# Attention scores turned onto key partitions, the maximum by way of TensorE, the quotient taken after the values

## The chip, the cores and the metric

One core of one Trainium2 chip runs the whole program. The metric is the device time of a launch in microseconds (us); the kernel before has a median of 992.38 us over 3 runs (990.18 to 994.85).

## The reference

Attention with the queries averaged in pairs, then a gated MLP on the tokens. There are 4 batches of 8 heads, 1152 keys and 576 averaged queries each, a head dimension of 64; the MLP goes from 512 to 2048 and back. All data is float32.

```python
q_pool = q.reshape(B, H, S // 2, 2, D).mean(axis=3)
scores = (1.0 / np.sqrt(D)) * np.matmul(q_pool, k.transpose(0, 1, 3, 2))
scores = scores - np.max(scores, axis=-1, keepdims=True)
attn = np.exp(scores)
attn = attn / (np.sum(attn, axis=-1, keepdims=True) + 1e-09)
x = np.matmul(attn, v)                      # then heads side by side: 2304 tokens x 512
h = x @ w_in                                # 2304 x 2048
g = h * np.clip(h + 3.0, 0.0, 6.0) / 6.0
return (g @ w_out).astype(np.float32)
```

The keys and queries are scaled by about 7.9 before, so the scores spread widely and the maximum matters.

## The kernel before, in words

**Precision.** A matmul on plain float32 is recorded as two matmul instructions. Where that is avoided, an operand is split into a rounded high part and a low part of type float32r (`upper_k`/`lower_k`, `take_q`, `split_x`, `convert`, `upper`/`lower`), and two or three products of rounded parts are added in PSUM.

**Attention.** The work goes by 16 pairs of heads (`g`). Keys and queries of a pair are loaded, pooled or split, turned by TensorE (`turn_k`, `turn_q`) and copied out of PSUM. A tile of scores has 128 queries on the partitions and 1152 keys along the row: nine tiles a pair, one of which (`None`) holds 64 queries of either head, its other half filled with zeros. `scores` makes a tile in three chunks of 384 keys. `least` (L392) moves a chunk out of PSUM, scaled by minus the scale, and carries the running minimum along the row; `expo` (L401) takes the exponential with that minimum as a bias and sums the row on the way; `recip` and `normal` (L407 to L412) divide the row by its sum on GpSimd. `turn` (L423) turns the result, 128 x 128 at a time, because the value product needs keys on partitions, and `take` (L306, L308) copies it into `pt`. `values` (L448) multiplies `pt` by the values, both heads side by side in one PSUM bank, for 320 or 256 queries at a time. `split_x` and `spill` write the two parts of x to DRAM.

**MLP.** Tokens go in chunks of 256 while attention runs: `layer` (L172, 12 matmuls of 256 columns), a gate on ScalarE and VectorE (L177, L181, L185, L190), and `project` (L205, 6 matmuls of 512 columns), for 16 blocks of 128 hidden features a chunk. One block of one chunk is one step `m`; there are 96. The last 768 tokens follow behind attention (L707 to the end). Before that, each block of weights is loaded raw, split into rounded parts by seven instructions (`convert`, L484 to L514, half of a block at a time) and written back to DRAM.

**Order.** The order of all instructions before L707 is written by the class `Order`: each step has a place (a priority), an estimated cost on its engine, the steps that it needs, and the buffers that it takes and frees. A list is worked through as if these estimates were times, and the order that comes out is held on every engine by dependencies. So each engine has one fixed queue. The constants at the top set the places: a pair lies 27 places after the one before it, block `f` of the weights at place 6 + 12.5 f, the MLP steps begin at place 112 and follow at 6.4 and later 3.15 places. SP issues all DMAs in its own place of that order.

**Buffers.** Up to the tile `WIDE` the scores have two double banks of PSUM (tag `v`), after it two single ones; the transposes have two banks, value products and weight splitting share one (tag `av`). `pt0` and `pt1` are single, score rows `s` have five buffers.

Of the kernel before, what the change touches and what calls it, by code (L numbers as in the profile page):

```python
# [113 lines left out]
def pooled_attention_then_gated_mlp(ctx, tc, q, k, v, w_in, w_out, out):  # L114
# [3 lines left out]
    P = 128  # L118
# [12 lines left out]
    REST = SQ % P  # L131
    QW = 2 * REST + SQ - REST
# [55 lines left out]
    def lower(pool, r6, gh, n):  # L188
        gl = pool.tile([P, n], F32R, tag="gl", name="gl")
        nc.vector.tensor_tensor(out=gl, in0=r6, in1=gh.bitcast(F32), op=ALU.subtract)  # L190
        return gl
# [46 lines left out]
    def second_part(early):  # L238
        front.close()
        ps_m["s"] = early.enter_context(tc.tile_pool(name="ps_s", bufs=2, space=PSUM))  # L240
# [4 lines left out]
    with ExitStack() as a:  # L245
        ld = a.enter_context(tc.tile_pool(name="ld", bufs=2))
        kq = a.enter_context(tc.tile_pool(name="kq", bufs=4 * KT // KC))
        sp = a.enter_context(tc.tile_pool(name="sp", bufs=5))
        sm = a.enter_context(tc.tile_pool(name="sm", bufs=6))
        tp = a.enter_context(tc.tile_pool(name="tp", bufs=1))  # L250
        vp = a.enter_context(tc.tile_pool(name="vp", bufs=2))
        xo = a.enter_context(tc.tile_pool(name="xo", bufs=2))
        ps_tr = a.enter_context(tc.tile_pool(name="ps_tr", bufs=2, space=PSUM))
        ps_av = a.enter_context(tc.tile_pool(name="ps_av", bufs=1, space=PSUM))

        q_t = []
        for n in range(2):
            both = []  # L260
            for nm in ("qh", "ql"):
                t = const.tile([P, 2, QW], F32R, name=f"{nm}{n}")
                for j in range(2):
                    z = slice(REST * (1 - j), REST * (2 - j))
                    nc.vector.tensor_copy(out=t[:, j, z], in_=zero.to_broadcast([P, REST]))
                both.append(t)
            q_t.append(both)

        TILES = [(None, 0)] + [(j, n) for n in range(SQ // P) for j in range(2)]
        EARLY = [(0, 0), (0, 1), (None, 0), (1, 0), (1, 1)] + TILES[5:]
        NTI = len(TILES)
        GROUPS = ((0, REST + 2 * P), (REST + 2 * P, SQ - REST - 2 * P))

        def tiles(g):
            return TILES if g else EARLY
# [3 lines left out]
        ps_t, s_t, cm_t, den_t, pt_t, av_t, xo_t = {}, {}, {}, {}, {}, {}, {}  # L281
# [44 lines left out]
        def near(g):  # L326
            return (ps_w, "tx") if g < NEAR else (ps_tr, "tr")

# [36 lines left out]
        def bank(i):  # L365
            return "v" if i < WIDE else "s"

# [395 lines left out]
```

## Time and profile before

| | |
|---|---|
| median of the runs | 992.38 us |
| span of the profiled execution, first to last instruction | 988.8 us |
| what a run's median has beyond that span | 3.6 us |
| PE (TensorE matmuls) busy | 942.5 us, 95%, 6288 instructions |
| DVE (VectorE) busy | 590.6 us, 60% |
| ACT (ScalarE) busy | 532.6 us, 54% |
| POOL (GpSimd) busy | 362.2 us, 37% |
| read from and written to DRAM | 171.97 and 30.93 MB |

Busy times are unions of instruction times. Matmuls overlap in the pipeline and their ends are modelled, so a PE that is shown busy is not one at its best pace; the distance from one matmul to the next is the better measure. The profile counts each plain float32 matmul of the value product as two records. For the profiled execution no time of its own is listed beside the span, so the median stands for it.

### The profile page before, as it was taken

What the parts mean: (1) busy time and instruction counts of PE and PEld (TensorE: products, weight loads), DVE (VectorE), ACT (ScalarE), POOL (GpSimd) and SP (SyncE); (2) the same over time, 40 slices, a digit from 0 to 9 for tenths busy, and PEclk for the clock granted to TensorE, in tenths of its full rate; (3) what the DMA queues carried; (4) which work ended last, traced back from release to release, by engine and by line L of the source; (5) the groups of instructions that cost most, each with busy time, mean ns of one, the idle gap of its engine ahead of it and who ended that gap; (6) DMA issues with size and microseconds to landing.
All of it is one profiled execution on the core that took longest, in us unless ns stands there. A gap on an engine that the chain in (4) does not pass through costs nothing.

```text
span 988.8 us, 17816 instructions
## 1 busy us (share of the span) xinstructions
PE 942.5 (95%) x6288; PEld 783.6 (79%) x6288; DVE 590.6 (60%) x1752; ACT 532.6 (54%) x1098; POOL 362.2 (37%) x338
## 2 busy tenths in 40 slices
PE   5898997999999999999999999999999999999997
PEld 4676676677678888888888878888898887788886
DVE  5787788678687766566575756566565552222222
ACT  4786786666565656455564555455564542222222
POOL 3876867545565434333251423323121110000000
PEclk9999997999999999999999999999999999999999
DMA  5875565788777476568475766557565668633332
GB/s 174 274 231 192 178 202 174 227 288 287 265 252 240 153 224 199 183 207 285 159 252 163 235 223 217 200 176 276 185 226 168 223 229 283 219 127 126 127 124 85
DMA packets 80888, 204.06 MB, mean 206 GB/s; under 512 B 7840, under 2 KB 31392, under 8 KB 80800
## 3 DMA queue, kind: packets, MB, share of 16 engines
q1 hardware_dynamic: 80800, 202.93, 62.6%
q8 instruction: 50, 0.82, 0.3%
q14 instruction: 38, 0.31, 0.1%
HBM read 171.97 MB, written 30.93 MB: 205 GB/s over the span
## 4 chain that ended last, share of the span: by engine, by line
PE 80%; DVE 9%; DMA 5%; ACT 3%; issue 2%; POOL 1%; SPq 0%; ACTq 0%; DVEq 0%; POOLq 0%
PE ph L172 18%; PE po L205 15%; PE pav L448 14%; PE pqk L384 13%; PE ptp L423 11%; PE pt L205 4%; DVE s L392 3%; DMA w<-w_d 3%; PE ptk L333 2%; PE ptq L346 1%; DVE gl L190 1%; DMA raw<-in_moe_w_in_dram 1%; DMA raw<-in_moe_w_out_dram 1%; ACT s L401 1%; DVE pcv L503 1%
## 5 line engine op out<-in xcount | busy, mean ns | idle before, releaser
L412 POOL TENSOR_SCALAR s<-s,den 128x1152 f32<-128x1152 f32 x144 | 177.8, 1235 | 340.1 <-DVE den L408 204.9
L423 PE MATMUL ptp<-ident,s 128*128 128x128 f32 x1296 | 209.1, 277 | 8.3 <-ACT pt L306 4.8
L401 ACT ACTIVATE s<-s,cm 128x1152 f32<-128x1152 f32 x144 | 181.7, 1262 | 40.7 <-DVE s L392 39.6
L384 PE MATMUL pqk<-kT,qh 128*128 128x384 f32 x480 | 184.9, 402 | 6.3 <-DVE s L392 5.2
L172 PE MATMUL ph<-mxmxh,w 128*128 128x256 f32 x896 | 184.3, 289 | 6.0 <-DMA w<-w_d 4.9
L423 PEld LDWEIGHTS ptp<-ident,s 128*128 128x128 f32 x1296 | 156.6, 142 | 39.2 <-issue 9.6
L306 ACT COPY pt<-ptp 128x384 f32<-128x384 f32 x296 | 138.7, 481 | 77.3 <-PE ptp L423 75.0
L392 DVE TENSOR_SCALAR_CACHE_REDUCE s<-pqk,cm 128x384 f32<-128x384 f32 x248 | 151.0, 609 | 32.0 <-PE pqk L384 27.7
L384 PE MATMUL pqk<-kT,ql 128*128 128x384 f32 x480 | 156.8, 343 | 0.0
L172 PEld LDWEIGHTS ph<-mxmxh,w 128*128 128x128 f32 x896 | 147.1, 191 | 11.5 <-DMA w<-w_d 4.5
L448 PE MATMUL pav<-pt,vr 128*64 128x256 f32 (+1 forms) x1152 | 149.2, 410 | 0.1
L205 PE MATMUL po<-w,gh 128*128 128x512 f32 x448 | 140.6, 395 | 0.0
L177 ACT ACTIVATE r<-ph,three 128x256 f32<-128x256 f32 (+1 forms) x128 | 63.8, 499 | 142.2 <-PE ph L172 141.9
L172 PE MATMUL ph<-mxmxl,w 128*128 128x256 f32 x448 | 126.7, 283 | 0.0
L448 PEld LDWEIGHTS pav<-pt,vr 128*64 128x64 f32 x1152 | 78.9, 137 | 56.7 <-issue 6.2
L181 DVE SCALAR_TENSOR_TENSOR r<-r,ph 128x256 f32<-128x256 f32 (+1 forms) x128 | 57.6, 450 | 97.8 <-ACT r L177 97.2
L308 DVE COPY pt<-ptp 128x384 f32<-128x384 f32 x136 | 74.9, 553 | 56.3 <-PE ptp L423 55.8
L392 DVE TENSOR_SCALAR_CACHE_REDUCE s<-pqk 128x384 f32<-128x384 f32 (+1 forms) x144 | 95.4, 662 | 16.6 <-PE pqk L384 15.0
L384 PEld LDWEIGHTS pqk<-kT,qh 128*128 128x128 f32 x480 | 89.1, 193 | 16.1 <-DVE s L392 11.4
L205 PE MATMUL po<-w,gl 128*128 128x512 f32 x224 | 93.5, 417 | 6.8 <-DVE gl L190 3.5
L205 PEld LDWEIGHTS po<-w,gh 128*128 128x128 f32 x448 | 84.8, 189 | 14.8
L190 DVE TENSOR_TENSOR gl<-r,gh 128x256 fp32r<-128x256 f32 (+1 forms) x128 | 79.1, 618 | 28.7 <-ACT gh L185 28.2
(55 smaller groups left out, 1132.8 us busy)
## 6 DMA issues: line engine op xcount, KB each, us to landing
w<-w_d SPq DMA_DIRECT2D x224, 512.0 KB, 4.6
w_d<-scratch SPq DMA_DIRECT2D x32, 512.0 KB, 3.7
kr<-in_k_dram SPq DMA_DIRECT2D x32, 288.0 KB, 4.6
qr<-in_q_dram SPq DMA_DIRECT2D x32, 288.0 KB, 4.8
vr<-in_v_dram SPq DMA_DIRECT2D x16, 576.0 KB, 5.3
raw<-in_moe_w_in_dram SPq DMA_DIRECT2D x16, 512.0 KB, 4.3
raw<-in_moe_w_out_dram SPq DMA_DIRECT2D x16, 512.0 KB, 4.3
mxmxh<-xh_d SPq DMA_DIRECT2D x7, 512.0 KB, 6.1
```

The source lines that it names most:

```text
L172: nc.tensor.matmul(ps, w[:, wi, cs], x[:, c, :], start=(m == 0), stop=(m == 3 * NCC - 1))
L177: nc.scalar.activation(out=r6, in_=ps, func=AF.Relu, bias=three)
L190: nc.vector.tensor_tensor(out=gl, in0=r6, in1=gh.bitcast(F32), op=ALU.subtract)
L205: nc.tensor.matmul(o, g[:, ts], w[:, wi, :], start=(f == 0 and n == 0), stop=(f == NFC - 1 and n == 2))
L306: nc.scalar.copy(out=out, in_=in_)
L308: by[eng].tensor_copy(out=out, in_=in_)
L384: nc.tensor.matmul(ps, x, kk.rearrange("p t k -> p (t k)"), start=(m == 0), stop=(m == len(ops) - 1))
L392: nc.vector.tensor_scalar(out=s[:, c * NK:end * NK].rearrange("p (c k) -> p c k", k=NK), in0=ps_t.pop((i, c))[0][:, 0:end - c, 0:NK], scal ...
L401: nc.scalar.activation(out=s, in_=s, func=AF.Exp, bias=cm_t.pop(i)[:, KC - 1:], scale=-1.0, accum_out=den_t[i])
L412: nc.gpsimd.tensor_scalar(out=s, in0=s, scalar1=den_t.pop(i), scalar2=1.0, op0=ALU.mult, op1=ALU.mult)
L423: nc.tensor.transpose(ps[:, x, :], s_t[i][:, o:o + P], ident)
L448: nc.tensor.matmul(av[j * D:(j + 1) * D, :], vr_t[g][:, j, t, :], pt_t[g, gr][:, t, j, :], start=(t == 0), stop=(t == KT - 1),)
```

## The change

Scores are made with keys on the partitions, so that what leaves the exponential is already what the value product needs, and `turn` and `take` go. A pair is cut into three thirds (`h`) of 192 queries, both heads side by side: one tile of scores has 128 keys by 2 x 192 queries, nine tiles a third, four matmuls of 192 columns each.

- `keep` (ACT) copies each tile out of PSUM; `most` (DVE) keeps a running maximum over the nine tiles, element by element.
- `fold`, `best`, `spread`: the maximum is turned by TensorE so that queries lie on partitions, reduced over the 128 that remain (DVE), and turned back from a broadcast operand, so that every partition holds the maximum of each query.
- `lessen` (DVE) subtracts it in place from three tiles at a time, `expo` (ACT) takes the exponential with the scale, without a bias and without a sum.
- `total` (POOL) adds up exponentials over tiles: two additions of 1152 columns that leave three tiles for the first six pairs, two more of 384 columns that leave one tile for the later ten. `denominators` sums over partitions with a matrix of ones, and so leaves the sum on every output row.
- `values` is as before, on 192 queries. `guard`, `recip`, `divide` take the quotient on its result; the low part of x is made by POOL and not by DVE.

The order has new steps and costs; a pair lies 26.9 places after the one before it, weight block `f` at place 13 + 9.3 f, MLP steps from place 99.5 in steps of 6.95 and 3.07, a projection 3.5 places behind its layer and not 1. POOL may take the gate's low half instead of DVE at a handicap of 12 places. PSUM has three banks for scores, one for the maximum, one for value products, three for turning keys and queries in the first four pairs and then the MLP's three.

```diff
-REC, NRM, TRN = 4, 4.5, 7
-AVL = 2
-FIRST, STEPS, LAG = 112, (6.4, 3.15), 1
-CONV, CSTEP = 6, 12.5
-NEAR = 5
-WIDE = 40
+SBUFS = 4
+FIRST, STEPS, LAG = 99.5, (6.95, 3.07), 3.5
+CONV, CSTEP = 13, 9.3
+NEAR = 4
+ADDS = (2, 4, 6)
+CUT = 2
+PER, AT, NGL = 26.9, (5.4, -6.8, 2.4, 14.5, -50, 27, 15.4), 12
...
+def adds(g, h):
+    return ADDS[0] if g < ADDS[2] else ADDS[1]
...
+        def scores(eng, g, h, t):
+            ps = ps_t[g, h, t] = ps_s.tile([P, 2, HQ], F32, tag="s", name="pqk")
+            for j in range(2):
+                for m, w in enumerate(q_t[g, h]):
+                    nc.tensor.matmul(ps[:, j, :], kT[g, j][:, t, :], w[:, j, :], start=(m == 0), stop=(m == 1))
+        def keep(eng, g, h, t):
+            if t == 0:
+                s_t[g, h] = sp.tile([P, KT, 2, HQ], F32, tag="s", name="s")
+            copy(eng, s_t[g, h][:, t], ps_t[g, h, t])
+        def most(eng, g, h, t):
+            if t == 1:
+                m_t[g, h] = sm.tile([P, 2, HQ], F32, tag="m", name="m")
+            m = m_t[g, h]
+            nc.vector.tensor_tensor(out=m, in0=ps_t[g, h, t], in1=s_t[g, h][:, 0] if t == 1 else m, op=ALU.max)
+        def fold(eng, g, h):
+            st = st_t[g, h] = ps_st.tile([P, 2 * TQ, P], F32, tag="m", name="pst")
+            m = m_t.pop((g, h)).rearrange("p j (t q) -> p (j t) q", q=QP)
+            for x in range(2 * TQ):
+                nc.tensor.transpose(st[:QP, x, :], m[:, x, :], ident)
+        def best(eng, g, h):
+            m_t["q", g, h] = sm.tile([QP, 2 * TQ], F32, tag="mq", name="mq")
+            nc.vector.tensor_reduce(out=m_t["q", g, h], in_=st_t[g, h][:QP], axis=AX.X, op=ALU.max)
+        def spread(eng, g, h):
+            mq = m_t.pop(("q", g, h))
+            st = st_t[g, h] = st_t[g, h].rearrange("p x k -> p (x k)")[:, 0:2 * HQ]
+            for x in range(2 * TQ):
+                nc.tensor.transpose(st[:, x * QP:(x + 1) * QP], mq[:, x:x + 1].to_broadcast([QP, P]), ident[:QP, :QP])
+        def third(g, h, c):
+            return s_t[g, h][:, KC * c:KC * (c + 1)].rearrange("p t j q -> p t (j q)")
+        def lessen(eng, g, h, c):
+            s = third(g, h, c)
+            nc.vector.tensor_tensor(out=s, in0=s, in1=st_t[g, h].unsqueeze(1).to_broadcast([P, KC, 2 * HQ]), op=ALU.subtract)
+        def expo(eng, g, h, c):
+            s = third(g, h, c)
+            nc.scalar.activation(out=s, in_=s, func=AF.Exp, scale=SCALE)
+        def total(eng, g, h, n):
+            if n == 0:
+                d_t[g, h] = dp.tile([P, KC, 2 * HQ], F32, tag="d", name="d")
+            d = d_t[g, h]
+            if n < 2:
+                out, x, y = d, third(g, h, 0) if n == 0 else d, third(g, h, n + 1)
+            else:
+                out, x, y = d[:, 0], d[:, 0], d[:, n - 1]
+            by[eng].tensor_tensor(out=out, in0=x, in1=y, op=ALU.add)
+        def denominators(eng, g, h, t0, t1):
             if t0 == 0:
+                pv = ps_av.tile([P, 512], F32, tag="av", name="pav")
+                av_t[g, h] = pv[:, HQ:2 * HQ], pv[:, 0:HQ]
+            den = av_t[g, h][0]
+            n = adds(g, h)
+            d = d_t.pop((g, h)).rearrange("p t (j q) -> p t j q", j=2) if n else s_t[g, h]
+            last = {0: KT, 2: KC, 4: 1}[n]
+            for t in range(t0, t1):
+                for j in range(2):
+                    nc.tensor.matmul(den[j * D:(j + 1) * D, :], ones, d[:, t, j, :], start=(t == 0), stop=(t == last - 1))
+        def values(eng, g, h, t0, t1):
+            av = av_t[g, h][1]
             for t in range(t0, t1):
                 for j in range(2):
                     nc.tensor.matmul(
+                        av[j * D:(j + 1) * D, :], vr_t[g][:, j, t, :], s_t[g, h][:, t, j, :],
                         start=(t == 0), stop=(t == KT - 1),
                     )
+        def guard(eng, g, h):
+            x_t[g, h] = xo.tile([P, HQ], F32, tag="x", name="x")
+            nc.scalar.activation(out=x_t[g, h], in_=av_t[g, h][0], func=AF.Copy, bias=EPS)
+        def recip(eng, g, h):
+            nc.vector.reciprocal(out=x_t[g, h], in_=x_t[g, h])
+        def divide(eng, g, h):
+            x = x_t[g, h]
+            nc.vector.tensor_tensor(out=x, in0=av_t.pop((g, h))[1], in1=x, op=ALU.mult)
+
...
+        def split_x(eng, g, h):
...
+                by[eng].tensor_tensor(out=xl, in0=x_t.pop((g, h)), in1=xh.bitcast(F32), op=ALU.subtract)
...
+                    add(("mm", g, h, t), z + t * step, {"PE": (376, 590)}, partial(scores, g=g, h=h, t=t),
+                        ([("mm", g, h, t - 1)] if t else [("mm", g, h - 1, KT - 1)] if h else [("mm", g - 1, NH - 1, KT - 1)] if g else [])
+                        + ([("el", g, h)] if not t else [])
+                        + [("ek", g, j, t // KC) for j in range(2)],
+                        ("sa", "sb"), (("q",) + (("kT", "kT") if h == NH - 1 else ())) if t == KT - 1 else ())
+                    add(("cp", g, h, t), z + t * step, {"ACT": (360, 440)}, partial(keep, g=g, h=h, t=t),
+                        [("mm", g, h, t)] + ([("cp", g, h, t - 1)] if t else []), () if t else ("S",), ("sa",) if t else ("sa", "sb"))
+                    if t:
+                        add(("mx", g, h, t), z + t * step + .1, {"DVE": (480, 560)}, partial(most, g=g, h=h, t=t),
+                            [("mm", g, h, t), ("mx", g, h, t - 1) if t > 1 else ("cp", g, h, 0)], ("m",) if t == 1 else (), ("sb",))
+                z += THIRD
+                add(("s1", g, h), z + AT[2], {"PE": (440, 660)}, partial(fold, g=g, h=h), [("mx", g, h, KT - 1)], ("st",), ("m",))
+                add(("s2", g, h), z + AT[2], {"DVE": (610, 690)}, partial(best, g=g, h=h), [("s1", g, h)])
+                add(("s3", g, h), z + AT[2], {"PE": (330, 550)}, partial(spread, g=g, h=h), [("s2", g, h)])
                 for c in C3:
+                    add(("su", g, h, c), z + AT[3] + 2 * c, {"DVE": (1280, 1360)}, partial(lessen, g=g, h=h, c=c),
+                        [("s3", g, h), ("cp", g, h, KT - 1)] + ([("su", g, h, c - 1)] if c else []), (), ("st",) if c == 2 else ())
+                    add(("ex", g, h, c), z + AT[3] + 1 + 2 * c, {"ACT": (1160, 1260)}, partial(expo, g=g, h=h, c=c), [("su", g, h, c)])
+                na = adds(g, h)
+                for n in range(na):
+                    cost = 2890 if n < 2 else 1040
+                    add(("ad", g, h, n), z + AT[4] + 2 * n, {"POOL": (cost, cost + 20)}, partial(total, g=g, h=h, n=n),
+                        [("ex", g, h, c) for c in (range(2) if n == 0 else (2,) if n == 1 else ())] + ([("ad", g, h, n - 1)] if n else []),
+                        () if n else ("d",))
+                z += AT[6] if na else AT[5]
+                parts = {0: KT, 2: KC, 4: 1}[na]
+                cuts = (0, 3, 6, KT) if g < CUT else (0, KT)
+                jobs = [(denominators, x, min(x + 3, parts)) for x in range(0, parts, 3)]
+                jobs += [(values, x, y) for x, y in zip(cuts, cuts[1:])]
+                for n, (fn, t0, t1) in enumerate(jobs):
+                    cost = 320 * (t1 - t0) + (190 if g < CUT or n == 0 else 0)
+                    add(("av", g, h, n), z + n, {"PE": (cost, cost + 220)}, partial(fn, g=g, h=h, t0=t0, t1=t1),
+                        [("av", g, h, n - 1)] if n else [("ad", g, h, na - 1) if na else ("ex", g, h, 2), ("lv", g)],
+                        () if n else ("av",), (("S",) + (("d",) if na else ()) + (("vr",) if h == NH - 1 else ()))
+                        if n == len(jobs) - 1 else ())
                 z += n
+                add(("gu", g, h), z + 1, {"ACT": (270, 350)}, partial(guard, g=g, h=h), [("av", g, h, len(jobs) - 1)], ("x",))
+                add(("rc", g, h), z + 1, {"DVE": (270, 340)}, partial(recip, g=g, h=h), [("gu", g, h)])
+                add(("dv", g, h), z + 1, {"DVE": (280, 360)}, partial(divide, g=g, h=h), [("rc", g, h)], (), ("av",))
+                add(("xh", g, h), z + 2, {"ACT": (260, 340)}, partial(split_x, g=g, h=h), [("dv", g, h)], ("xo",))
+                add(("xl", g, h), z + 2, {"POOL": (580, 600)}, partial(split_x, g=g, h=h), [("xh", g, h)], (), ("x",))
...
-            add(("gl", m), z, {"DVE": (400, 490)}, partial(do_lower, m=m), [("gh", m)], (), ("r6",))
+            add(("gl", m), z, {"DVE": (400, 490), "POOL": (740, 760, NGL)}, partial(do_lower, m=m), [("gh", m)], (), ("r6",))
```

## Rows read from the trace of the kernel before

**Rows 1.** Chain of waits cut to two stretches, 50 to 188 and 344 to 826 us, by line.
```profile
by line: PE pav L448 23.6%; PE ptp L423 15.7%; DVE s L392 13.7%; PE pqk L384 13.4%; DVE pcv L503 4.9%; issue 4.9%; DMA raw<-in_moe_w_out_dram 4.0%; DVE scratch L507 3.5%; DVE pcv L498 2.5%; DVE pt L308 2.5%; PE ptk L333 2.2%; DVE ql L357 1.
...
by line: PE po L205 22.1%; PE ph L172 19.2%; PE pqk L384 17.4%; PE pav L448 16.9%; PE ptp L423 15.3%; DVE gl L190 2.2%; PE ptk L333 1.8%; PE ptq L346 1.5%; DVE s L392 1.0%; issue 0.7%; ACT pt L306 0.4%; ACT s L401 0.4%; ACT gh L185 0.3%; DV
```

**Rows 2.** Windows by stage: length; PE, PEld, DVE, ACT, POOL busy; clock, DMA share, GB/s.
```profile
50.00:188.00 138.00, 125.97 (x868) 95.08 (x864) 104.32 (x297) 102.42 (x210) 99.72 (x98) 0.96 0.60 194
...
344.00:826.00 482.00, 477.68 (x3381) 407.86 (x3379) 290.56 (x922) 260.68 (x544) 149.68 (x129) 1.00 0.65 213
826.00:988.80 162.80, 153.95 (x797) 131.47 (x795) 44.23 (x82) 43.56 (x82) 0.00 (x0) 0.98 0.46 150
```

**Rows 3.** Windows by stage, line 384 alone: length, PE and PEld busy (instructions).
```profile
50.00:188.00 138.00, 59.40 (x222) 36.02 (x222) 0.96 0.60 194
188.00:344.00 156.00, 47.15 (x180) 28.46 (x180) 1.00 0.76 250
344.00:826.00 482.00, 133.28 (x500) 79.26 (x500) 1.00 0.65 213
```

**Rows 4.** Windows by stage, line 172 alone, same columns.
```profile
188.00:344.00 156.00, 28.45 (x204) 25.50 (x204) 1.00 0.76 250
344.00:826.00 482.00, 118.61 (x868) 109.70 (x868) 1.00 0.65 213
```

**Rows 5.** Chain of waits, 600 to 612 us: start us, us, what.
```profile
600.41 4.04 PE pav L448 x36
...
604.85 1.41 PE po L205 x6
606.26 0.33 PE ptp L423 x3
...
606.95 0.21 PE ptk L333 x3
...
607.90 1.43 PE ph L172 x12
609.33 0.25 PE ptq L346 x3
...
609.90 0.71 PE pqk L384 x4
```

**Rows 6.** Timeline of DVE, 90 to 97 us: start us, us, instruction.
```profile
93.64 0.69 DVE L503 SCALAR_TENSOR_TENSOR pcv<-raw,pcv 128x512 uint32<-128x512 uint32 x1
94.23 0.95 DVE L392 TENSOR_SCALAR_CACHE_REDUCE s<-pqk 128x768 f32<-128x768 f32 x1
```

**Rows 7.** Timeline of DVE, 609 to 616 us.
```profile
612.59 0.55 DVE L308 CAST kT<-ptk 128x384 fp32r<-128x384 f32 x1
613.06 0.54 DVE L308 COPY pt<-ptp 128x384 f32<-128x384 f32 x1
...
614.44 0.95 DVE L190 TENSOR_TENSOR gl<-r,gh 128x256 fp32r<-128x256 f32 x1
```

**Rows 8.** Timeline of POOL, the same stretch.
```profile
613.68 1.42 POOL L322 TENSOR_TENSOR ks<-kr,ks 128x576 fp32r<-128x576 f32 x1
```

**Rows 9.** Timeline of all engines, 643.6 to 647 us, two lines.
```profile
644.12 0.42 DVE L190 TENSOR_TENSOR gl<-r,gh 128x256 fp32r<-128x256 f32 x1
...
646.00 1.23 POOL L412 TENSOR_SCALAR s<-s,den 128x1152 f32<-128x1152 f32 x1 [9.24 <-DVE den L408]
```

**Rows 10.** Groups of instructions, POOL: count | busy us, mean ns | idle before.
```profile
L314 POOL TENSOR_TENSOR qp<-qr 96x384 f32<-96x384 f32 x60 | 61.2, 1031 | 51.0 <-PE ptq L346 50.9
...
L514 POOL TENSOR_TENSOR scratch<-scratch 128x512 fp32r<-128x512 f32 x32 | 41.2, 1287 | 13.3 <-ACT scratch L306 11.9 <-POOL s L412 1.2
```

**Rows 11.** Groups of instructions, DVE, same columns.
```profile
L408 DVE RECIPROCAL den<-den 128x1 f32<-128x1 f32 x144 | 23.6, 164 | 5.0
...
L460 DVE TENSOR_TENSOR xl<-pav,xh 128x320 fp32r<-128x320 f32 x16 | 7.8, 490 | 46.4 <-ACT xh L457 46.4
```

**Rows 12.** Windows by stage, line 190 alone: length, DVE busy (instructions).
```profile
344.00:826.00 482.00, 47.26 (x73) 1.00 0.65 213
```

More of the change, by code (lines that the diff above doesn't have):

```diff
@@ L246, in pooled_attention_then_gated_mlp @@
         ld = a.enter_context(tc.tile_pool(name="ld", bufs=2))
[L247 to L250, printed above, removed]
+        kq = a.enter_context(tc.tile_pool(name="kq", bufs=4))
+        qq = a.enter_context(tc.tile_pool(name="qq", bufs=3))
+        sp = a.enter_context(tc.tile_pool(name="sp", bufs=SBUFS))
+        sm = a.enter_context(tc.tile_pool(name="sm", bufs=2))
+        dp = a.enter_context(tc.tile_pool(name="dp", bufs=2))
         vp = a.enter_context(tc.tile_pool(name="vp", bufs=2))
         xo = a.enter_context(tc.tile_pool(name="xo", bufs=2))
-        ps_tr = a.enter_context(tc.tile_pool(name="ps_tr", bufs=2, space=PSUM))
+        ps_s = a.enter_context(tc.tile_pool(name="ps_s", bufs=3, space=PSUM))
+        ps_st = a.enter_context(tc.tile_pool(name="ps_st", bufs=1, space=PSUM))
         ps_av = a.enter_context(tc.tile_pool(name="ps_av", bufs=1, space=PSUM))
[L258 to L277, printed above, removed]
+        NH = 3
+        HQ = SQ // NH
+        TQ = QT // NH
+        ones = const.tile([P, D], F32, name="ones")
+        nc.vector.memset(ones, 1.0)
         C3 = range(KT // KC)
         kr_t, vr_t, ks_t, kT, qr_t, qp_t, tr_t = {}, {}, {}, {}, {}, {}, {}
-        ps_t, s_t, cm_t, den_t, pt_t, av_t, xo_t = {}, {}, {}, {}, {}, {}, {}
+        ps_t, s_t, m_t, st_t, d_t, av_t, x_t, xo_t, q_t = {}, {}, {}, {}, {}, {}, {}, {}, {}
         def pair(g, j):
@@ new lines, in take_k, with turn_q, take_q @@
+            copy(eng, kT[g, j][:, KC * c:KC * (c + 1), :], tr_t.pop(("k", g, j, c)))
+        def turn_q(eng, g, h):
+            ps = tr_t["q", g, h] = space(g, 2, HQ)
+            for j in range(2):
+                for t in range(TQ):
+                    src = qp_t[g, j][:, h * TQ + t, :, :].rearrange("p r d -> p (r d)")
+                    nc.tensor.transpose(ps[:, j, t * QP:(t + 1) * QP], src, ident[:QP, :QP])
+        def take_q(eng, g, h):
+            ps = tr_t["q", g, h]
+            if eng == "ACT":
+                q_t[g, h] = [qq.tile([P, 2, HQ], F32R, tag=t, name=t) for t in ("qh", "ql")]
+                nc.scalar.copy(out=q_t[g, h][0], in_=ps)
+            else:
+                qh, ql = q_t[g, h]
+                nc.vector.tensor_tensor(out=ql, in0=ps, in1=qh.bitcast(F32), op=ALU.subtract)
```

233 lines of the change are left out of this document (50 added, 183 removed).

## The prediction, before the changed kernel ran

> **What bounds the kernel now.** I read the windows by stage first, then the chain of waits inside two of the stages, and only then rows of single instructions. The run has three parts. Up to 188 us TensorE (PE) does attention alone; from there attention and the MLP steps run together, the weight splitting ending some way into it; from 826 us on only the MLP is left. The reader is to see that the share of PE climbs from 126 of 138 us to 478 of 482 while the Vector engine (DVE) falls from 104 of 138 to 291 of 482 [rows 2]. The chain says the same: in the middle part it is nearly all PE lines, and in the first part DVE lines and a DMA stand between PE's [rows 1]. So a microsecond of PE work is worth most between 344 and 826 us, less before 188, and nothing of the change lies behind 826.
>
> The pace comes from counts. A pair of heads has 60 score matmuls on line 384, so the first part does 222/60 = 3.7 pairs in 138 us (37.3 us a pair), and the middle part 8.33 pairs with 868/12 = 72.3 MLP steps [rows 3, 4]. In the chain of a busy stretch, where PE runs without a gap, three transposes of P cost 0.33 us, four score matmuls 0.71, 36 records of a value product 4.04, three key transposes 0.21, three query transposes 0.25 and an MLP step 1.43 + 1.41 = 2.84 [rows 5]. One pair needs of PE 27 x 0.33 + 30 x 0.355 + 9.1 (576 columns at the rate of the 256 in 4.04) + 6 x 0.21 + 4 x 0.25 = 30.9 us. Then the middle part held 8.33 x 30.9 + 72.3 x 2.84 = 463 us of work in 482, 96%; the first part 3.7 x 30.9 = 114 in 138, 83%. These two shares are my yardsticks for how far a leading engine is filled here.
>
> **PE, part by part.** Removed: 27 transposes of P a pair on three chunks, 27 x 0.33 = 8.9 us. Scores: 30 pairs of 384 columns become 108 matmuls of 192. Matmuls of 256 columns come 0.119 us apart (12 in 1.43), of 384 0.177 [rows 5], that is 0.45 ns a column; 192 columns should come 0.091 apart, 9.8 us a pair against 10.7. No row shows a matmul of this type under 256 columns: the lower end is that estimate, the upper end twice it, the rate at which the plain float32 transposes of P go (0.110 for 128 columns). I take the estimate, since the transposes of the rounded type take 0.070 for 128 columns with a weight load each. The Trainium skill ("TensorE: Matmul & The Clock Gate", LDWEIGHTS) prices a load of 128 columns at columns over 1.2 GHz, 107 ns, and by that the loads and not the columns would set 192-column matmuls, 18 us more over the later pairs; the row of 0.21 for three loads and transposes disagrees, so it changes no term here. Values keep their 576 columns a head, 9.1 us. Added: the denominators, 0.337 us for a tile of both heads (three quarters of 4.04/9), nine tiles a pair in the first six pairs (3.0 us) and three later (1.0); the fold, 12 transposes of 128 columns at 0.110 (1.3); the spread, 12 of 96 columns at 0.083 (1.0). Key and query transposes stay at 1.3 and 1.0. Sum: 26.5 us for the first six pairs, 24.5 for the later ten, so 4.4 and 6.4 less a pair, 90 us in all.
>
> **DVE.** Neighbouring 384-column instructions start 0.47 us apart (612.59 to 613.06), 512-column ones 0.59, and the durations 0.55, 0.69 and 0.95 for 384, 512 and 768 columns give 1.04 ns a column [rows 6, 7]. So a subtraction of 1152 columns takes about 1.27, one of 192 columns 0.27. A pair will have 24 maxima x 0.47 = 11.3, 9 subtractions x 1.27 = 11.4, 3 reductions of 512 columns x 0.59 = 1.8, 6 small ones (reciprocal, product) x 0.27 = 1.6, query differences and some key copies 2.4: 28.5 us. The reciprocal is shown only for one column, 0.164 us [rows 11]; its ends are 0.27 and 1.27 (the price of six times its columns), and I take the low one, since 0.55 - 383 x 0.00104 = 0.15 us is what any DVE instruction here has left for one column. Splitting the weights adds 6 x 0.59 per block of rows; the block spacing falls from 12.5 to 9.3 places of the plan, so 2.9 blocks fall on a pair: 10.3 us. Together 38.8 us a pair for the first six pairs (13 + 16 x 9.3 = 162 places of 26.9 a pair). Now DVE is busy 104.3/3.7 = 28.2.
>
> **GpSimd (POOL)** loses the normalising (one 1152-column instruction a tile) and gets the sums. Two-input work goes from 1031 ns for 384 columns to 1287 for 512 [rows 10], 2.0 ns a column, so a 1152-column add is about 2.6 us. Early: 6 adds 15.6, pooling and key splitting 8, the low halves of x 2, weights 2.9 x 2 x 2.1 (1.29 for the two-input step [rows 10], half of it for the one-input step, a part of the casts) = 12: 38 us a pair. Later: 22 of adds and 10 others, 32 us. ACT changes copies of P for copies of scores, drops the accumulator reads and gets two short copies per third; it was busy 102 of 138 and 261 of 482 [rows 2], and I take it as hidden. If that cover were gone it would show in the same stage as DVE.
>
> **The first six pairs** therefore change their leader: DVE 38.8 and POOL 38, PE 26.5. At 83% of the leader that is 46.7 us a pair, at 96% 40.4; I take 90%, 43.1, between the two yardsticks, because two engines nearly tie. Start-up: 280 of 960 score matmuls were done by 188 us (180 and 500 follow [rows 3]), so 188 - 4.67 x 37.3 = 14 us, kept. About 7 MLP steps fit beside pairs five and six; their DVE share adds 5 us. First part: 14 + 6 x 43.1 + 5 = 278 us (261 to 299).
>
> **The later ten pairs** are PE's: 10 x 24.5 = 245, and of the 89 MLP steps done when attention ends today (17 + 72) 82 are left, 233: 478 us, at 96% 498 (493 to 520). Waits that are new stand here. The fold waits on PE for the last maximum, the spread for the reduction; score tiles and MLP matmuls are queued behind them. If PE stood through the 0.69 us reduction each time, 30 thirds would cost 21 us; if the order always has other work between, nothing. I take nothing beyond the 4% already idle and keep 520 as the far end. Score banks come free only when ACT and DVE have both read them; three are there. The low half of x moves behind POOL's adds, so a spill, and on SP the weight loads behind it, can be 5 us late; three weight buffers cover about 9 us of MLP steps alone, more when attention is interleaved. The one bank for value products is shared with the weight splitting: three holds of about 5.3 us and 5.8 of about 2 a pair, 27 of 43 us.
>
> **The last part** keeps 163 us [rows 2]. Sum: 278 + 498 + 163 = 939 for the span. The span was 988.8 and the median of the runs 992.4, 3.6 around it: **943 us**, 5% less.
>
> **The rivals.**
> B, the saving passes whole: DVE keeps up and PE leads from the start. 90/0.96 = 94 off: 898. For it: PE is the chain's largest part early too [rows 1]. Against: 38.8 us of DVE do not fit in 37.3.
> C, the early part eats the gain: DVE is filled only as far as today, 76% [rows 2], 51 us a pair, 325 + 498 + 163 + 4 = 990, no change. For: conversions and adds tie DVE and POOL. Against: today DVE is not the leader.
> D, slower: the long adds on POOL lock out the one DVE instruction with two SBUF inputs, line 190. Its 0.42 us with POOL idle [rows 9] become 0.95 when POOL's key split is running and end just after it [rows 7, 8]. If each met a whole add, 0.42 + 2.6 = 3.0, DVE would have 10 x 28.5 + 82 x (0.33 for the gate, by the same 1.04 ns a column, + 3.0) = 558 us in the middle part, 581 at 96%: 278 + 581 + 163 + 4 = 1026. It decides from a mean of 2.0 us, where 285 + 82 x 2.35 passes PE's 478; today the mean is 0.65 (47.3 us for 73 in the middle part) [rows 12]. At POOL's future load, 320 of 498 us, I work out about 1.1, so it should not decide. The new maxima and subtractions have one input in PSUM, and so has line 460's, which keeps 490 ns [rows 11]. The Trainium skill ("SBUF — State Buffer", Who interferes with whom) has the same lock: a DVE instruction with two SBUF inputs and a GpSimd one that reads SBUF exclude each other for a whole instruction. Here the trace agrees, 0.95 against 0.42.
> E: 192-column matmuls run at half rate: 10 x 108 x 0.091/0.96 = 102 more, 1045.
>
> **Chances.** Forecast 0.50 (own range 921 to 986), B 0.20, C 0.15, D 0.10, E 0.05. The range of 8 in 10 goes from B's 895 to just past C, 997, leaving out D, E and a little of C. About 0.5%, or 5 us, is what can be told from no change. Faster: forecast and B, with 0.04 of C, 0.74; same 0.08 of C; slower D, E and 0.03 of C, 0.18.
>
> **What would show it.** Right: windows before about 280 us with DVE near 90% and PE clearly below its present share, the granted clock (0.96 there now) perhaps lower; the chain there by DVE lines; the stretch behind it 95% PE work with about 50 us a pair; no more than 1.3 us for line 190's instruction; 192-column matmuls in steps near 0.09. Wrong: an early pace under 39 or over 48 us a pair, PE waiting for DVE at the fold, the spread or a score bank in the middle part, or score matmuls above 0.11.

## The result and the profile after

The changed kernel takes 980.17 us (977.92 to 983.33), the kernel before 991.38 in the same rounds: a ratio of 0.988 [0.9845, 0.991], 1.2% faster where 5% was forecast. The time lies inside the range and the sign is right; the size is not: 37 us of the gain are missing.

The page of the kernel after: busy time by engine, then the slices of PE, DVE and the granted clock.

```profile
PE 923.9 (94%) x7056; PEld 805.9 (82%) x7056; DVE 720.1 (74%) x1093; ACT 581.3 (59%) x1134; POOL 535.3 (55%) x406
...
PE   6888889889898999999999999999999999999997
...
DVE  5989998887899998886876786788887875322222
...
PEclk9799888999999999999999999999999999999999
```

PE is still the busiest engine. The slices of DVE show 8 and 9 at the start and fall to 6 to 8 later, as forecast; the granted clock is between 0.7 and 0.9 in slices 2 and 5 to 7, behind slices in which PE was busy for six or eight tenths, and 0.9 or more from the eighth, 171 us, on.

Windows of all engines by stage, with the columns of [rows 2]. The cut at 281 is near the forecast end of the sixth pair.

```profile
14.00:281.00 267.00, 236.92 (x1883) 204.01 (x1882) 233.60 (x355) 193.81 (x368) 185.69 (x142) 0.90 0.64 207
281.00:826.00 545.00, 533.03 (x4363) 470.77 (x4362) 436.72 (x646) 340.12 (x678) 344.43 (x255) 1.00 0.71 226
826.00:979.50 153.50, 147.22 (x776) 124.92 (x775) 43.43 (x78) 41.20 (x78) 1.34 (x2) 0.99 0.45 144
```

Line 352, the score matmuls (line 384 before, [rows 3]), 108 of them to a pair, from the start to 282 us and in the middle stage:

```profile
0.00:282.00 282.00, 110.98 (x648) 92.38 (x648) 0.91 0.65 210
...
281.00:826.00 545.00, 159.19 (x1084) 141.12 (x1084) 1.00 0.71 226
```

and for line 175, the first half of an MLP step (line 172 before, [rows 4]), 12 to a step:

```profile
281.00:826.00 545.00, 135.85 (x996) 124.12 (x996) 1.00 0.71 226
```

All 648 score matmuls of the first six pairs are done at 282 us (forecast 278). The 545 us from 281 on hold 1084/108 = 10.04 pairs and 996/12 = 83 MLP steps; 498 us were forecast for 10 pairs and 82 steps. So nearly the whole miss stands behind 281. The last part is 153.5 us instead of 163, since a few more steps are done when it begins.

Groups of instructions of the kernel after, columns as in [rows 10]:

```profile
L386 DVE TENSOR_TENSOR s<-s,pst 128x1152 f32<-128x1152 f32 x144 | 193.6, 1346 | 11.3 <-PE pst L379 10.9
...
L400 POOL TENSOR_TENSOR d<-d,s 128x1152 f32<-128x1152 f32 x48 | 128.7, 2680 | 5.9 <-ACT s L390 4.2
...
L428 DVE RECIPROCAL x<-x 128x192 f32<-128x192 f32 x48 | 64.6, 1346 | 17.5 <-ACT x L425 17.3
```

The subtraction of 1152 columns (forecast a step of 1.27; the row gives 1346 ns from start to end) and POOL's add (forecast 2.6, row 2.68) came as worked out. In the chain the fold takes 0.44 for four transposes and the spread 0.33, also as forecast. Two did not: the reciprocal of 192 columns takes 1346 ns, as long as a subtraction of six times its columns, and 1.27 us in the chain, the high one of the two ends that were drawn from [rows 11]; the two denominator matmuls of a tile, four records of line 412, take 0.48 us in the chain, not 0.34. The third miss is in the timeline of PE, which shows the steps between score matmuls (start us, us, instruction):

```profile
521.50 0.25 PE L352 MATMUL pqk<-qh,kT 128*128 128x192 f32 x1
521.59 0.27 PE L352 MATMUL pqk<-ql,kT 128*128 128x192 f32 x1
521.70 0.28 PE L352 MATMUL pqk<-qh,kT 128*128 128x192 f32 x1
521.81 0.27 PE L352 MATMUL pqk<-ql,kT 128*128 128x192 f32 x1
```

After the first step, 0.09, they start 0.11 us apart, not 0.091. "Above 0.11" stood in the prediction as a sign that it is wrong.

### The profile page after: what moved, and what is told of

Same layout as the page of the kernel before. It is cut to its first block, busy times and chain, and to the rows that moved or that the text cites. A ratio compares the mean times of both kernels' runs of the same rounds, so it can differ in the third digit from the quotient of the medians.

```text
span 979.5 us, 18765 instructions
## 1 busy us (share of the span) xinstructions
PE 923.9 (94%) x7056; PEld 805.9 (82%) x7056; DVE 720.1 (74%) x1093; ACT 581.3 (59%) x1134; POOL 535.3 (55%) x406
## 4 chain that ended last, share of the span: by engine, by line
PE 67%; DVE 16%; ACT 6%; issue 6%; DMA 4%; SPq 0%; POOL 0%; DVEq 0%; ACTq 0%
PE ph L175 17%; PE pqk L352 13%; PE po L208 12%; PE pav L418 12%; DVE m L363 6%; PE pt L208 4%; PE pav L412 3%; DVE x L428 3%; ACT s L293 2%; DVE gl L193 2%; PE pt L325 2%; PE pst L379 1%; DVE s L386 1%; DMA w<-w_d 1%; ACT s L390 1%
## 5 line engine op out<-in xcount | busy, mean ns | idle before, releaser
L352 PE MATMUL pqk<-qh,kT 128*128 128x192 f32 x864 | 232.7, 300 | 27.1 <-DVE m L363 19.7
L293 ACT COPY s<-pqk 128x384 f32<-128x384 f32 x432 | 200.0, 481 | 73.9 <-PE pqk L352 47.1
L363 DVE TENSOR_TENSOR m<-pqk,m 128x384 f32<-128x384 f32 x336 | 184.8, 550 | 54.9 <-ACT s L293 42.6
L352 PE MATMUL pqk<-ql,kT 128*128 128x192 f32 x864 | 218.6, 283 | 0.0
L352 PEld LDWEIGHTS pqk<-qh,kT 128*128 128x128 f32 x864 | 171.4, 198 | 56.1 <-DVE m L363 31.7
L386 DVE TENSOR_TENSOR s<-s,pst 128x1152 f32<-128x1152 f32 x144 | 193.6, 1346 | 11.3 <-PE pst L379 10.9
L390 ACT ACTIVATE s<-s 128x1152 f32<-128x1152 f32 x144 | 168.1, 1170 | 24.0 <-DVE s L386 23.2
L352 PEld LDWEIGHTS pqk<-ql,kT 128*128 128x128 f32 x864 | 172.8, 200 | 2.6
L418 PE MATMUL pav<-s,vr 128*64 128x192 f32 x1728 | 153.2, 332 | 0.0
L400 POOL TENSOR_TENSOR d<-d,s 128x1152 f32<-128x1152 f32 x48 | 128.7, 2680 | 5.9 <-ACT s L390 4.2
```

What stands on the lines that cost most here:

```text
L293: nc.scalar.copy(out=out, in_=in_)
L352: nc.tensor.matmul(ps[:, j, :], kT[g, j][:, t, :], w[:, j, :], start=(m == 0), stop=(m == 1))
L363: nc.vector.tensor_tensor(out=m, in0=ps_t[g, h, t], in1=s_t[g, h][:, 0] if t == 1 else m, op=ALU.max)
L386: nc.vector.tensor_tensor(out=s, in0=s, in1=st_t[g, h].unsqueeze(1).to_broadcast([P, KC, 2 * HQ]), op=ALU.subtract)
L390: nc.scalar.activation(out=s, in_=s, func=AF.Exp, scale=SCALE)
L400: by[eng].tensor_tensor(out=out, in0=x, in1=y, op=ALU.add)
```

## Experiments

The theory: two prices were wrong, the reciprocal (48 x 1.00 us more on DVE, 1.27 for 0.27) and the step of the score matmuls (1728 x 0.02 us more on PE), and work done by the engines is what the time lacks. Rivals: the written order, planned with estimates that are too low for both, places the work badly (order); or the first part is slow for want of balance between splitting and attention (balance). Ratios are to the kernel before, with their intervals.

**e1_no_recip.** The quotient is left out: a maximum of the same shape stands in for the reciprocal.

```diff
-            nc.vector.reciprocal(out=x_t[g, h], in_=x_t[g, h])
+            nc.vector.tensor_tensor(out=x_t[g, h], in0=av_t[g, h][0], in1=x_t[g, h], op=ALU.max)
```

> The changed kernel with its 48 reciprocals of 192 columns (1.35 us each on DVE) replaced by a maximum of the same shape with one PSUM input; the quotient is left out. The changed kernel took 980.2. Theory A (the reciprocal, five times as long as forecast, holds DVE and with it PE in the later pairs): the instruction falls to 0.35 us, DVE loses about 48 us, the 30 us that its line has in the chain of waits mostly go, 950 to 965 us. Rival B (DVE has room, PE's own work is longer than forecast and is the bound): 974 to 980.

Measured: 960.3 us (959.1 to 962.4), 0.970 [0.9676, 0.9723]: 20 us less than the kernel after. Line 352 in e1, up to the end of the sixth pair:

```profile
0.00:270.50 270.50, 106.83 (x648) 89.26 (x648) 0.92 0.68 219
```

Then all engines from the sixth pair's last score matmul to the last value product, in the kernel after

```profile
282.00:831.50 549.50, 537.53 (x4408) 474.47 (x4407) 437.53 (x649) 340.74 (x680) 344.17 (x255) 1.00 0.71 226
```

and in e1:

```profile
270.50:809.20 538.70, 533.83 (x4408) 474.00 (x4406) 406.40 (x648) 343.45 (x679) 344.18 (x255) 1.00 0.71 231
```

Six pairs are done at 270.5 us instead of 282, and the later ten, with the same 4408 matmul records, take 539 us instead of 549.5. So about half of what the reciprocal costs lies in the first part and half behind it. The chain of waits by line, 344 to 826 us, of the kernel after:

```profile
by line: PE pqk L352 18.6%; PE ph L175 18.4%; PE po L208 17.6%; PE pav L418 15.9%; DVE x L428 4.0%; DVE m L363 3.8%; PE pav L412 2.5%; DVE gl L193 2.0%; ACT s L293 2.0%; issue 2.0%; PE pt L325 1.9%; PE pst L379 1.8%; DVE s L386 1.3%; DVE r 
```

and of e1:

```profile
by line: PE ph L175 23.3%; PE po L208 23.0%; PE pqk L352 22.1%; PE pav L418 17.2%; PE pav L412 2.7%; PE pt L325 2.4%; PE pst L369 2.2%; PE pst L379 1.7%; PE pt L337 1.4%; DMA w<-w_d 1.4%; DVE gl L193 0.8%; SPq L222 0.4%; DVE m L363 0.3%; AC
```

The lines of DVE and ACT nearly vanish. A piece of the chain of the kernel after shows why; up to the second maximum, the same sequence stands there seven times between 344 and 826 us (start us, us, what; steps of under 0.05 and one issue of 0.24 left out):

```profile
517.59 0.51 PE pqk L352 x4
...
518.12 0.49 ACT s L293
518.63 0.56 DVE m L363
519.19 1.27 DVE x L428
520.48 0.37 DVE x L432
...
521.13 0.48 ACT r L180
...
521.63 0.43 DVE r L184
...
522.09 0.42 ACT gh L188
...
522.53 0.63 DVE gl L193
523.16 0.48 DVE m L363
...
523.69 0.44 PE pt L325 x3
```

The maximum follows ACT's copy of a score tile; the reciprocal stands behind it on DVE for 1.27 us; the product waits for the reciprocal, ACT's cast of x for the product, and behind the cast stand the steps of an MLP gate, ACT and DVE in turn, then the next maximum, and only then a bank for PE's key transposes. Yet PE had other work beside most of it. By the counts of lines 352 and 175 the pace between 344 and 826 us is 93% filled (at 26.7 us a pair and 2.84 a step) in the kernel after and 94% in e1, a few us, though the chain gives 94 of 482 us to other engines in the one and 21 to other engines and DMAs in the other.

**e3_half_load.** The low part of the queries meets only 64 of the 128 keys of a tile (the rest of that product is left out), so every second score matmul loads half the weights over the same columns.

```diff
-                    nc.tensor.matmul(ps[:, j, :], kT[g, j][:, t, :], w[:, j, :], start=(m == 0), stop=(m == 1))
+                    n = P if m == 0 else D
+                    nc.tensor.matmul(ps[0:n, j, :], kT[g, j][:, t, 0:n], w[:, j, :], start=True, stop=True)
```

> The changed kernel with the second of every two score matmuls made on 64 of the 128 keys, so that its weight load has 64 columns; it overwrites instead of adding, so the scores lack a part. Theory L (the score matmuls come 0.11 us apart because a load of 128 columns takes that long, whatever the 192 columns of the matmul): the step behind a half load falls to about 0.09, PE has 864 x 0.02 = 17 us less to do, 10 of them in the later pairs, 965 to 973 us. Rival M (the matmul itself takes 0.11): the step stays, 977 to 983.

Measured: 969.98 us (965.87 to 970.98), 0.979 [0.9759, 0.9815]: 10 less than the kernel after. The timeline of PE in e3:

```profile
503.54 0.25 PE L353 MATMUL pqk<-qh,kT 128*128 128x192 f32 x1
503.63 0.25 PE L353 MATMUL pqk<-ql,kT 128*64 128x192 f32 x1
503.72 0.28 PE L353 MATMUL pqk<-qh,kT 128*128 128x192 f32 x1
503.83 0.25 PE L353 MATMUL pqk<-ql,kT 128*64 128x192 f32 x1
```

The matmul behind one with a half load starts after 0.09, the one behind a whole load after 0.11 (but for the first step of the group, as above), with the same 192 columns. So the weight columns set the step, not the columns that are moved. Half the weight columns mean half the load and also half the rows of the result; e3 and e4 halve both together. That it is the load and not the rows is argued and not shown.

**e4_ladder.** A program of its own, which computes none of the reference: 24 matmuls in a row for each size, and reciprocals of 1 to 384 columns.

> Nothing of the reference: 24 matmuls of the rounded type in a row for each of seven pairs of weight columns and moving columns (128x512, 128x384, 128x256, 128x192, 64x192, 128x96, 64x96), twice, and four reciprocals each of 1, 48, 96, 192 and 384 columns. Theory L: 128x192 and 128x96 both come about 0.11 us apart, 64x192 0.09, 64x96 about 0.055; the wider ones 0.227, 0.175, 0.12. Rival M: 64x192 as 128x192, and 128x96 clearly below. Reciprocal: 0.16, 0.46, 0.76, 1.35, 2.5 us if it is a fixed part and 6.2 ns a column.

Its groups of reciprocals:

```profile
L46 DVE RECIPROCAL y<-raw 128x384 f32<-128x384 f32 x4 | 10.2, 2553 | 0.1
...
L46 DVE RECIPROCAL y<-raw 128x192 f32<-128x192 f32 x4 | 5.4, 1353 | 0.1
...
L46 DVE RECIPROCAL y<-raw 128x96 f32<-128x96 f32 x4 | 3.0, 753 | 0.1
...
L46 DVE RECIPROCAL y<-raw 128x1 f32<-128x1 f32 x4 | 0.7, 163 | 0.1
```

(2553 - 163)/383 = 6.24 ns a column, all the way from one column. And its timeline, the 24 matmuls of 64 weight columns by 192, 128 by 96 and 64 by 96 (start us, us for all):

```profile
22.10 2.28 PE L42 MATMUL p64x<-x 128*64 128x192 f32 x24
24.22 2.80 PE L42 MATMUL p128x<-x 128*128 128x96 f32 x24
26.86 1.56 PE L42 MATMUL p64x<-x 128*64 128x96 f32 x24
```

With the last one's own duration (0.25, 0.27, 0.22 by their groups) taken off, the 23 steps are 0.088, 0.110 and 0.058 us. Whole loads give 0.110 with 96 columns, and the matmuls with 192 are busy just as long:

```profile
L42 PE MATMUL p128x<-x 128*128 128x192 f32 x48 | 5.6, 273 | 0.0
L42 PE MATMUL p128x<-x 128*128 128x96 f32 x48 | 5.6, 273 | 0.0
```

Halving the moved columns does nothing, halving the weight columns does.

**e2_costs.** Only the order's own estimates are set to the measured costs; the work is the same.

```diff
-                    add(("mm", g, h, t), z + t * step, {"PE": (376, 590)}, ...
+                    add(("mm", g, h, t), z + t * step, {"PE": (448, 660)}, ...
...
-                add(("rc", g, h), z + 1, {"DVE": (270, 340)}, ...
+                add(("rc", g, h), z + 1, {"DVE": (1270, 1340)}, ...
```

> The changed kernel with only the order's estimates corrected: 1270 ns for the reciprocal on DVE and 448 for the four score matmuls, where 270 and 376 stood; every instruction stays as long as it is. Theory O (most of the loss is that the order expects these steps to be short, so other engines stand when they are not): 958 to 968. Theory W (the work itself is the loss, 48 us of DVE and 39 of PE more than forecast): 974 to 984.

Measured: 976.47 us (974.62 to 980.76), 0.986 [0.9828, 0.9888]. At most 4 us, and the interval overlaps that of the kernel after. So the order holds a small part of the missing gain at most.

**e5_lnexp** computes the same quotient on ACT as exp(-ln(den)):

```diff
-            nc.scalar.activation(out=x_t[g, h], in_=av_t[g, h][0], func=AF.Copy, bias=EPS)
+            nc.scalar.activation(out=x_t[g, h], in_=av_t[g, h][0], func=AF.Ln, bias=tiny)
...
-            nc.vector.reciprocal(out=x_t[g, h], in_=x_t[g, h])
+            nc.scalar.activation(out=x_t[g, h], in_=x_t[g, h], func=AF.Exp, scale=-1.0)
```

> The changed kernel with the quotient's reciprocal made on ACT as exp(-ln(sum)), both functions from one table; the order's cost for that step is put on ACT. Theory A: as without reciprocals, less what 48 instructions of about 0.35 us cost on ACT: 950 to 968 us. Rival B: 974 to 985.

Measured: 969.08 us (966.0 to 971.64), 0.979 [0.9755, 0.9826]: 11 less than the kernel after, 1 above the expected range. Groups of e5:

```profile
L428 ACT ACTIVATE x<-pav,tiny 128x192 f32<-128x192 f32 x48 | 20.1, 420 | 48.5 <-PE pav L421 48.2
...
L431 ACT ACTIVATE x<-x 128x192 f32<-128x192 f32 x48 | 17.7, 368 | 0.5
...
L146 ACT ACT_TABLE_LOAD x1 | 1.3, 1283 | 0.7 <-PEq L727 0.7
```

The logarithm takes the place of ACT's guarding copy (0.33 us in the kernel after), so 0.46 us more on ACT replace 1.35 on DVE, with one table load in the whole run. This gets about half of e1's gain. **e8_lnexp_costs** adds e2's corrected estimates to it.

> The reciprocal as exp(-ln(sum)) on ACT, and the order told what the traces show: 448 for four score matmuls, 330 and 270 for the two short ACT instructions. Theory O: 955 to 963, below the 969 of that version without it. Theory W: 966 to 972.

Measured: 967.57 us (965.96 to 971.26), 0.977 [0.9738, 0.9795]: no difference from e5 that these rounds can tell. Again no gain is seen from the order.

**e6_both** is e1 and e3 together.

> The changed kernel with both edits: the maximum in place of the reciprocal, and every second score matmul on 64 of the 128 keys (quotient and a part of the scores left out). If the two mis-sized terms are all that the forecast of 943 missed, the two gains add (980 to 960 and 980 to 970) and the time is 946 to 953; half of the load excess, about 1080 x 0.01 = 11 us in the later pairs, stays in. Rival: the two hide behind each other or a third cause holds the rest: 957 or more.

Measured: 945.89 us (942.77 to 947.74), 0.954 [0.9506, 0.957]. The savings add up: 20 + 10 were seen alone, 34 together, and with both the time is within 3 us of the forecast. Half of the excess load is still in it, so this nearness is partly luck: its six pairs are done at 267 us, 11 before the forecast, and the rest takes 677 us of the span, 16 more than the 661 that were forecast.

**e9_splitting** tests balance: the weight splitting starts sooner and its blocks stand further apart, as in the kernel before.

```diff
-CONV, CSTEP = 13, 9.3
+CONV, CSTEP = 6, 12.5
```

> The changed kernel with one part undone: the weight blocks are split at the places of the kernel before (6 + 12.5 f, not 13 + 9.3 f). If DVE leads the first six pairs, as forecast, a pair there is lighter by 0.75 blocks x 6 x 0.59 = 2.7 us of DVE: six pairs done at about 270 instead of 281, the splitting ends later, past 380 us, and the total is 975 to 985. Rival: PE leads there, six pairs at 279 to 283, and MLP steps wait for weights: over 985.

Measured: 997.12 us (990.01 to 999.15), 1.0045 [1.0019, 1.007], slower than the kernel before. It does not decide what it was meant to: by 281 us it had split only one block less, so DVE was hardly relieved, and the pace of the first part stayed. What it shows is the other end. MLP matmuls of line 175 between 281 and 400 us, in the kernel after

```profile
281.00:400.00 119.00, 21.47 (x156) 19.43 (x156) 1.00 0.70 225
```

and in e9

```profile
281.00:400.00 119.00, 16.78 (x120) 15.56 (x120) 0.94 0.63 207
```

and its chain by line, 200 to 400 us:

```profile
by line: PE pqk L352 12.7%; PE pav L418 9.8%; issue 8.2%; PE po L208 8.0%; DMA w<-w_d 7.8%; PE ph L175 7.6%; DVE m L363 7.4%; PE pav L412 4.1%; ACT s L293 3.0%; DMA w_d<-scratch 2.9%; DVE x L428 2.7%; DVE gl L193 2.4%; DVE s L386 2.4%; DMA 
```

Ten steps against thirteen, the clock at 0.94, and 7.8% of the chain waits for weights. Splitting ended at 358 us instead of 334, and steps that could have stood beside attention were late. The denser splitting is part of what the change gains, at this spacing of the other steps.

**e10_blocks, e11_blocks_only, e12_blocks_early** use the cause. The three thirds of queries of the two heads are cut into six blocks of 192 columns, and a third now takes two blocks of one head where it can, so one load of keys serves 384 columns: 1152 score matmuls instead of 1728. In e10 the blocks go in order of heads, on top of e8; e11 does the same with the reciprocal left on DVE; e12 takes e10 with the blocks that the first MLP steps need put first.

```diff
+        BLOCKS = (((0, 0), (0, 1)), ((0, 2), (1, 0)), ((1, 1), (1, 2)))
...
+            if j == jj:
+                for m, w in enumerate(q_t[g, h]):
+                    nc.tensor.matmul(ps.rearrange("p j q -> p (j q)"), kT[g, j][:, t, :], w.rearrange("p j q -> p (j q)"), start=(m == 0), stop=(m == 1))
+                return
```

> The version with exp(-ln(sum)) and corrected estimates (968), and a pair cut otherwise: six blocks of one head by 192 queries, two neighbours to a third, so that two of three thirds hold one head and need two matmuls of 384 columns a key tile instead of four of 192; each spill has four DMAs for two. Theory L: 72 matmuls of 0.111 us a pair become 36 of 0.175, 1.7 us a pair less on PE, 17 in the later pairs: 946 to 956 us. Rival S (the loads are hidden behind other waits, or SP's extra DMAs hold up x and the weights): 964 or more.

> The changed kernel with only that other cut of a pair; the reciprocal stays on DVE and the order's costs stay. Theory L: PE has 1.7 us a pair less, 962 to 970 us, if DVE's reciprocals leave PE the room as they did for half loads. Rival S: 975 or more.

Measured: e10 980.38 us (975.66 to 980.94), 0.990 [0.988, 0.9918], 13 us slower than e8; e11 975.4 (970.45 to 977.5), 0.984 [0.9807, 0.987], no more than 5 better than the kernel after. The reason is seen in the MLP matmuls (line 176) of e10 between 188 and 222 us:

```profile
188.00:222.00 34.00, 0.24 (x1) 0.19 (x1) 0.85 0.54 168
```

One, where e8 had 36: the first MLP rows now need all three thirds of a pair, and the early attention has that many fewer MLP matmuls beside it. e12 tests that.

In e12 the edit to e10 is

```diff
-        BLOCKS = (((0, 0), (0, 1)), ((0, 2), (1, 0)), ((1, 1), (1, 2)))
+        BLOCKS = (((0, 0), (0, 1)), ((1, 0), (1, 1)), ((0, 2), (1, 2)))
```

> As the version with blocks, exp(-ln(sum)) and corrected estimates, but the blocks in an order in which the first two thirds hold the first 384 queries of one head each and the last third the rest of both, so that the first MLP chunk of 256 tokens needs two thirds and not three; a spill of the last third has two DMAs again. If the blocks lost their gain because the first MLP step moved from 208 to 222 us and PE stood meanwhile, it comes back: MLP from about 208, 946 to 958 us, below the 968 without blocks. If the loads' saving is worth nothing in the later pairs: 964 or more.

Measured: 962.32 us (955.71 to 963.36), 0.971 [0.9687, 0.9738], the fastest version with the whole result, 18 us under the kernel after and 5 under e8, whose interval it touches. It lies between the two ranges that were expected. The same window and line in e12, and then two of its groups:

```profile
188.00:222.00 34.00, 3.60 (x26) 3.24 (x27) 0.96 0.73 235
```

```profile
L357 PE MATMUL pqk<-qh,kT 128*128 128x384 f32 x288 | 114.4, 397 | 19.9 <-DVE m L372 11.8 <-ACT s L297 4.6 <-ACT kT L297 2.4
...
L361 PE MATMUL pqk<-qh,kT 128*128 128x192 f32 x288 | 75.1, 291 | 10.3 <-DVE m L372 7.6 <-ACT s L297 1.5 <-DVE ql L350 0.6
```

The steps are back early, and half the score matmuls take 384 columns. Against e10 18 us are won, but not by the order of the blocks alone: the last third's x goes out in two pieces again. At a step of 0.177 for 384 columns [rows 5] against 2 x 0.111 the wider matmuls save 576 x 0.045 = 26 us of PE; 5 were got. From 344 to 826 us its chain has 2.3% for the spill of x, which still goes out in more pieces than in e8; whether that is all of it was not tried.

## Why the prediction was right in sign and wrong in size

**The step that failed first: "I take the low one" for the reciprocal.** Its only row was for one column, and 163 ns are there again in e4; what was argued from it, that 0.15 us is the fixed part and the columns cost what others cost, had no row behind it. The Trainium skill ("VectorE: DVE Perf Modes", First, the fixed hardware budget) says that a reciprocal runs as an iterated divide with a repeat count of 8; it gives no time, but it speaks against the low end, and e4 shows a column at 6.24/1.04 = 6 times another's. In the chain it takes 1.27 us, so 48 x 1.00 = 48 us more of DVE than forecast. e1 puts its price at 20 us by the medians, and between the two profiled executions at 12 in the first part (282 against 270.5 us) and 11 behind it.

**The second: the step of 0.091 for score matmuls.** It took two rates from matmuls of 256 and 384 columns, where the columns last longer than a load, and carried them on to 192, where they don't. The row of 0.21 for three loads and transposes [rows 5] was used against the load's price, and it was the wrong kind of instruction: most such groups still last 0.22 in e1, while matmuls with loads of as many columns stand 0.111 apart; a load of 128 columns is recorded with 0.15 us for a key transpose and with 0.20 for a score matmul (means in the kernel after). The Trainium skill ("TensorE: Matmul & The Clock Gate", LDWEIGHTS), set aside there with its 107 ns, was right for this case: e4 shows 0.110 for 96 and 192 columns, and 0.058 for half the load. Rival E had the place and too large a size: over ten pairs the floor costs 10 x 108 x 0.02 = 22 us, not 102.

**The rest of the later part.** From 282 us to the last value product it took 549.5 us for ten pairs and 84 MLP steps. At the prediction's prices that is 245 + 84 x 2.84 = 484 of work, 504 at its 96%: a miss of 46. The reciprocal holds 11 of them, since e1 needs 539 for the same matmuls. In the chain of e1, which stays on PE, the pieces between 344 and 826 us give what is left: a score matmul 0.119 on average where the chain goes on with PE (0.111 within a run), 108 x 0.028 = 3.0 us a pair over the forecast, the 22 us included; denominators 3 x 0.14 = 0.4; key transposes 0.28 a group on average, 0.4; values 3.08 instead of 3.03, 0.15. Together 4.0 a pair, 40 us. That makes 524 of work in e1's 539, 97%, so 5 us go back because PE stands less than the 4% that were taken: 11 + 40 - 5 = 46. The idle time is what is left over, so this sum closes by itself; the terms after the reciprocal are read from the chain and not shown by an experiment, but for e3's 10 us for half of the load's excess. Why a score matmul costs 0.008 more than its load when it follows other work stays open.

**The first part** came out near its forecast, 282 for 278, partly by luck, because errors offset each other. Without the reciprocal it would have been 270: only 13 of the 16 blocks are split by then (26 instructions of line 477, two to a block) where all 16 were put down, three blocks of 3.5 us of DVE; and 10 MLP steps are done, not 7. The chain of the kernel after, 14 to 281 us, by line:

```profile
by line: issue 13.8%; PE pav L418 13.3%; PE pqk L352 12.7%; DVE m L363 11.0%; PE pav L412 7.6%; PE ph L175 4.3%; DMA raw<-in_moe_w_in_dram 3.2%; ACT s L293 3.1%; DVE x L428 3.1%; PE po L208 2.9%; DMA mxmxl<-xl_d 2.6%; DVE pcv L477 2.1%; ACT
```

DVE's lines stand in it, but PE's hold more, and PE is busy 237 of 267 us, 89%. The same window of the kernel before, where PE has 92%:

```profile
14.00:281.00 267.00, 244.87 (x1647) 189.21 (x1646) 202.65 (x586) 186.25 (x386) 176.17 (x170) 0.98 0.69 228
```

These are two marks of the forecast that failed. DVE still weighs most there, as far as the runs tell: it is busy 234 us, 87% where 90% was taken, and relieving it alone (e1) moved the sixth pair by 12 us, while PE's work at its prices (5.9 x 28.7 for the pairs with the load floor, and 10 x 2.84) fills 197 of 267 us. But those prices are of the full clock, 2.4 GHz, and the granted clock is 0.90 there against 0.98 before, so PE is at 1.2 GHz for about a fifth of the window. In the chain a value product of 36 records takes 3.79 us at 164 us, where 0.79 is granted, and 3.08 at 514 us, where 1.00 is. The prediction named a lower clock and put no price on it; what it costs in the first part no run separates. From 281 to 826 us 1.00 is granted, so the larger miss is not the clock's.

The sum of the miss, then: +4 in the first part, +46 from there to 826 us (544 for 498), -9.5 in the last part, whose steps were done sooner: 40 us on 939.

**Rivals.** The time came between the forecast and C's 990, but not by C's mechanism: the early part did not eat the gain. D did not decide; line 193 (190 before, [rows 12]), on DVE and POOL from 281 to 826 us:

```profile
281.00:826.00 545.00, 59.81 (x58) 17.67 (x24) 1.00 0.71 226
```

59.81/58 = 1.03 us on DVE, forecast 1.1, its price of 2.0 not reached; and 24 of these instructions went to POOL, where the prediction left all 82 on DVE. B is excluded by e1, where DVE's relief alone moved the early pairs. The fold and the spread, taken at nothing beyond PE's own work, stand in e1's chain only with PE's own lines (369 and 379, 2.2 and 1.7%), so their waits were hidden there. The waits of PE that the prediction named as a sign of being wrong are there in the kernel after, but short: from 344 to 826 us PE stands 3.0 us for DVE and ACT at score matmuls, 2.2 for DVE at key transposes and 1.3 at the spread.

## What to carry to other kernels

Price an instruction by a row of its own kind and size, and let the high end stand for a new one until a row exists: a row for one column says nothing of the cost of a column, and a transpose says nothing of a matmul. When cutting matmuls into narrower ones, count weight loads, not columns: below the width at which the columns outlast the load, the narrower matmul costs the same. Two operands that share their weights can be placed side by side, but the order of the work decides what that gives: 13 us lost in e10, 5 won in e12. A line's share of the critical chain is not what its removal gives, if the engine it returns to had other work meanwhile: the reciprocal has 8 us of the chain of the first part (3.1%) and 19 from 344 to 826 us (4.0%), and its removal gave 12 and 11. Count the work done in the stretch instead.

## What was not expected of the hardware

A reciprocal on DVE costs 6.24 ns a column against 1.04 for the other operations there, with the same 0.16 us for one column: 753 ns for 96, 1353 for 192, 2553 for 384. Matmuls of the rounded type with 128 weight columns follow each other at 0.110 us in a run, at 96 as at 192 columns, while three transposes, whose loads have 128 columns too, last 0.22 together. ACT's ln and exp of 192 columns need 420 and 368 ns with one table load in the run, 1283 ns.
